# Second layer's down-projection turned to token columns, with DVE block transposes at the end and an earlier scan schedule

## The chip, the cores and the metric

One core of one Trainium2 chip runs the whole program. The metric is device microseconds (us) of one execution; smaller is better. Engines are named as in the profile: PE (TensorE matmul), PEld (its weight load), DVE (VectorE), ACT (ScalarE), SP (the queue from which nearly all DMAs are issued).

## The reference

Three stages follow each other on 12160 tokens (2 sequences of 6080) of width 256:

```python
f = lower_bound + (1 - lower_bound) * sigmoid(f_logit)
h = f[:, t] * h + (1 - f[:, t]) * x[:, t]        # a scan over 6080 steps
y1 = relu(h @ w_in1)**2 @ w_out1                 # 256 -> 2048 -> 256
y2 = elu(y1 @ w_in2) @ w_out2                    # 256 -> 2048 -> 256
```

Weights arrive in 64-bit floats, everything else in 32-bit floats, and the output is 32-bit.

## The kernel before, in words

**Tiling.** Tokens are cut into 24 blocks: 384 tokens, then 23 of 512 (`FIRST`, `block_sizes`). A layer `m` (0 is the squared relu, 1 the elu) treats one block in 8 groups `g` of 256 hidden units. One (layer, block, group) is called a slot here. A float product is made of three matmuls of high and low parts (`(wh,gh)`, `(wh,gl)`, `(wl,gh)`), each pair of parts made by a copy that rounds (`high_part`) and a subtraction (`low_part`). The first four blocks of layer 0 are `plain`: 12 first products of full width. All other slots form the first product from seven half-size products, 9 matmuls named `first` and 12 named `later` (line 626), with sums on DVE around them.

**One slot of layer 1**, engine by engine: PE `first` into a PSUM tile `pc` (2 buffers); ACT `snap` copies three quarters of it (654); PE `later`; DVE `common` (662), `mid_blocks` (669), `pair` (657), `last_block` (665); ACT `first_block` (672), `below` (682), `exp` (685); DVE `elu` (688); ACT `high_part` (693); DVE `low_part` (698), which gives `g` (3 buffers); PE `out_mm` (725), the second product, which stands three slots later in PE's order. Layer 0 has relu and square on ACT in place of `below`, `exp` and `elu`.

**The second product.** For layer 0 weights are stationary and activations move: 12 matmuls with 512 moving columns a slot, results `acc` with output channels on partitions. For layer 1 it is the other way round: 128 tokens of `g` are stationary and 256 columns of `wo` move, 24 matmuls a slot, so that `acc` has tokens on partitions and can be stored as it is: `add_evacuation` moves it by ACT (805) and stores rows of 1 KB (809). Layer 0's result goes through DRAM (`xd`) and comes back by `add_reload`.

**The scan.** `add_scan` works on half a block: four DMAs each for `fs` and `xs` (549, pieces of 256 bytes), tanh on ACT (553), two DVE block transposes to channels on partitions (558), gate, feed, two scans (564, 572, 585). `fs`, `xs`, `fT` and `xT` had one buffer each.

**What sets the order.** Blocks go in pairs; runs of 16 slots alternate between layer 1 of one pair and layer 0 of a pair two ahead, after two runs of layer 0 at the start. `class Order` holds every step with its cost, due time, reads and writes, and lays them out engine by engine with costs of its own (`act`, `dve`, `SAME`, `CROSS`, `LOAD`, `HOLD`); the result is a fixed order in each engine's queue. `SPREAD` says how many slots ahead of its pair's layer-0 run the transposes of each of the four half-block scans are released, so all four fall into the layer-1 run before. I call the runs of layer 1 that have scans to do loaded. Weights are made in the kernel from their 64-bit words (`add_weights`, 383 to 415), those of layer 1 during the first 250 us; `add_sums` and `add_kept_parts` build the seven half-size weights and keep them in DRAM, from where `add_stream` loads them for each run.

Of the kernel before, what the change touches and what calls it, by code (L numbers as in the profile page):

```python
# [7 lines left out]
F32 = mybir.dt.float32  # L8
# [4 lines left out]
ALU = mybir.AluOpType  # L13
# [4 lines left out]
HB = 256  # L18
FIRST = (384,)
LAST = ()  # L20
# [6 lines left out]
START = 12.0  # L27
SPREAD = (15, 11, 8, 4)

BUFS = {  # L30
    "fs": 1, "xs": 1, "fT": 1, "xT": 1, "F": 2, "xA": 1, "xB": 1, "ws": 4, "wp": 3, "r": 3, "e": 1,
    "g": 3, "s": 2, "st": 3, "a": 5, "o": 2, "pc": 2, "acc": 4,
}
# [13 lines left out]
class Order:  # L47
# [8 lines left out]
    RATE, AHEAD = 240.0, 2.0  # L56
    HOLD = 0.2
    SLACK = 0.3
# [35 lines left out]
    def run(self):  # L94
# [33 lines left out]
        while any(ready.values()):  # L128
# [14 lines left out]
            if e == "SP":  # L143
                moved = max(moved, t0 + us / 2) + s[6] / self.RATE
                free[e] = max(free[e], moved - self.AHEAD)
                ends[n] = (e, max(moved, t0 + us))
            else:
                ends[n] = (e, t0 + us)
            for r in ready.values():
# [12 lines left out]
def kernel(  # L162
# [26 lines left out]

    late = ctx.enter_context(tc.tile_pool(name="late", bufs=1))  # L190
    wo1 = late.tile([P, KF, 2, D], F32R, name="wo1")
    pools = {"ws": ctx.enter_context(tc.tile_pool(name="ws_pool", bufs=BUFS["ws"]))}
# [5 lines left out]
    warm = const.tile([P, 1], F32, name="warm")  # L198
    wo = [const.tile([P, KF, 2, D], F32R, name="wo0"), wo1]
    pools |= {  # L200
# [165 lines left out]
    def add_weights(i, m, kind, c, due, wk=None):  # L366
        t = {}

        def load(e):
            t["st"] = new("st", [P, 2, CE // 2, 2], I32)  # L370
            load_w(nc.scalar if i == 0 else nc.sync, t["st"], m, kind, c)
            if i == 0:
                for k in range(KD):
                    nc.scalar.dma_start(lb[:, k : k + 1], lower_bound.rearrange("(q c i o) -> c q i o", q=4, c=KD, o=1)[k])
                nc.scalar.activation(warm, warm, AF.Exp)
            sv = t["st"].rearrange("p k e w -> p (k e) w")
            t["low"], t["high"] = sv[:, :, 0], sv[:, :, 1]
# [19 lines left out]

        def parts():
            if kind == 0:
                return t["a"], ws_t[m, c][:, 0, 0:4], ws_t[m, c][:, 1, 0:4]  # L400
            v = t["a"].rearrange("p (k e) i -> p k (e i)", k=2)
            return v, *(wo[m][:, 2 * c : 2 * c + 2, x, :] for x in range(2))

        def high_part(e):
            if kind == 0:
                ws_t[m, c] = new("ws", [P, 2, NW, P], F32R)
            v, hi, _ = parts()
            if e == "ACT":
                nc.scalar.activation(hi, v, AF.Copy)
            else:  # L410
                nc.vector.tensor_copy(hi, v)

        def low_part(e):
            v, hi, lo = parts()
            nc.vector.tensor_tensor(lo, v, hi.bitcast(F32), op=ALU.subtract)

# [3 lines left out]
        def keep_whole(e):  # L420
# [3 lines left out]
        steps = [  # L424
            ["SP", 0.1 if i == 0 else 1.9 if m == 0 and kind == 0 else 0.475, load, (), [st], None, 512],
            ["ACT", act(CE), scaled, [st], [a]],
# [8 lines left out]
        if m == 1 and kind == 0:  # L435
# [7 lines left out]
            *steps,  # L443
            ["DVE", dve(CE, True), high_part, [a], [w], ("ACT", act(CE))],
            ["DVE", dve(CE), low_part, [a], [w]],
        ])
        if kind == 0:
            order.add("SP", 0.5, due + 6.0, keep, [w], [("wd", m, c, 0)], None, 512)
            order.add("SP", 0.5, due + 3.0, keep_whole, [a], [("rd", c)], None, 256)

# [33 lines left out]
    def add_parts(m, b, ready, due):  # L484
# [132 lines left out]
    def add_slot(i, m, b, g, wk):  # L617
# [82 lines left out]
        def out_mm(e):  # L700
# [3 lines left out]
            for j in (2 * g + 1, 2 * g):  # L704
                d = 0 if j % 2 else 2 * n
                gh, gl = (t["g"][:, x, d : d + 2 * n] for x in range(2))
                one, two = begin and j % 2 == 1, end and j % 2 == 0
                for q in range(KD if m == 0 else 2 * n // P):
                    if m == 0:
                        if one:  # L710
                            acc_t[m, b].append(pa.tile([P, TB], F32, tag="acc", name="acc"))
                        a = acc_t[m, b][q][:, : 2 * n]
                        wh, wl = (wo[0][:, j, x, q * P : (q + 1) * P] for x in range(2))
                        three = ((wh, gh), (wh, gl), (wl, gh))
                        clear = one
                    else:
                        if one and q % 2 == 0:
                            acc_t[m, b].append(pa.tile([P, TB], F32, tag="acc", name="acc"))
                        a = acc_t[m, b][q // 2][:, q % 2 * D : (q % 2 + 1) * D]
                        vh, vl = (x[:, q * P : (q + 1) * P] for x in (gh, gl))  # L720
                        wh, wl = (wo[1][:, j, x, :] for x in range(2))
                        three = ((vh, wh), (vh, wl), (vl, wh))
                        clear = one and q % 2 == 0
                    for k, (u, v) in enumerate(three):
                        nc.tensor.matmul(a, lhsT=u, rhs=v, start=clear and k == 0, stop=two and k == 2, skip_group_check=True)  # L725

        na = KD if m == 0 else -(-2 * n // HB)
        if g == 0:
# [52 lines left out]
    def add_evacuation(m, b):  # L781
        n = sizes[b]
        due = out_due[m, b, KG - 1] + 12 * ROW * n + 4.0
        for q, key in enumerate(acc_k[m, b]):
            if m == 0:
                k = ("o", o_n[0] + q)

# [4 lines left out]
                def spill(e, q=q):  # L792
                    nc.sync.dma_start(xd[b][:, q], o_t[m, b, q])

                chain(due, [
                    ["ACT", act(n, True), move, [key], [k]],
                    ["SP", 0.5, spill, [k], [("xd", b, q)], None, n // 2],
                ])
            else:
                k = ("o", o_n[0] + q)  # L800
                w = min(2, n // P - 2 * q)

                def move(e, q=q, w=w):
                    o_t[m, b, q] = new("o", [P, 2, D])
                    nc.scalar.activation(o_t[m, b, q][:, :w], acc_t[m, b][q].rearrange("p (i e) -> p i e", i=2)[:, :w], AF.Copy)

                def store(e, q=q, w=w):
                    t0 = starts[b] + q * 2 * P
                    nc.sync.dma_start(out[t0 : t0 + w * P, :].rearrange("(i p) e -> p i e", p=P), o_t[m, b, q][:, :w])

                chain(due, [
                    ["ACT", act(w * D, True), move, [key], [k]],
                    ["SP", 0.5, store, [k], (), None, w * 128],
                ])
        o_n[0] += len(acc_k[m, b])

# [104 lines left out]
```

## Time and profile before

| | |
|---|---|
| runs | 2083.47, 2083.7, 2085.03 us, median 2083.7 |
| the profiled execution | 2083.75 us, of which its span is 2082.0 |
| busy in the span | PE 2034.5, PEld 1925.6, DVE 1732.3, ACT 1697.1 us |
| mean granted TensorE clock | 0.996 of 2.4 GHz |
| DMA | 268.10 MB, 16 engines 41.3% busy |

Busy PE is modelled and overlaps, so a share near 100% says that PE is rarely empty, not how fast it goes. How fast it goes is read from the distance between starts of neighbouring groups.

### The profile page before, as it was taken

Reading aid. Unit: us, or ns where it says so; the run is one execution under the profiler, and the core shown is the slowest. Engines: PE = TensorE matmul, PEld = TensorE weight load, DVE = VectorE, ACT = ScalarE, POOL = GpSimd, SP = SyncE. Lnnn points to the kernel's source line nnn. Section 1 sums busy time; section 2 is a strip of 40 time slices with the busy share of each in tenths; the row PEclk is TensorE's granted clock in tenths of the full one; section 3 lists DMA queues with packets and bytes.
Section 4 is the critical chain, followed back from the end, with each engine's and each line's share of the span. In section 5 each row is a group of like instructions: output and inputs, shape, how many; then the busy total and the mean of one; then the engine's idle time right before and its main releaser. Section 6 shows DMA issues by size and latency. Waiting matters only on the chain.

```text
span 2082.0 us, 36897 instructions
## 1 busy us (share of the span) xinstructions
PE 2034.5 (98%) x14640; PEld 1925.6 (92%) x14640; DVE 1732.3 (83%) x2830; ACT 1697.1 (82%) x2149; POOL 0.2 (0%) x4
## 2 busy tenths in 40 slices
PE   3999999999999999999999999999999999999998
PEld 3888889999999999999999999999999999999998
DVE  7977996996897798699699689779869968967876
ACT  5887778888888888889788888888888878888886
POOL 0000000000000000000000000000000000000000
PEclk8999999999999999999999999999999999999999
DMA  8787452442343344334244234334433424423321
GB/s 220 229 258 237 143 173 89 128 131 93 124 141 102 119 116 134 116 108 144 89 124 136 92 124 140 105 119 115 135 117 106 140 90 122 133 92 130 104 95 39
DMA packets 207540, 268.10 MB, mean 129 GB/s; under 512 B 110984, under 2 KB 135944, under 8 KB 207368
## 3 DMA queue, kind: packets, MB, share of 16 engines
q1 hardware_dynamic: 206784, 265.21, 40.7%
q8 instruction: 116, 1.90, 0.4%
q10 hardware_dynamic: 584, 0.53, 0.1%
q14 instruction: 56, 0.46, 0.1%
HBM read 221.91 MB, written 43.78 MB: 128 GB/s over the span
## 4 chain that ended last, share of the span: by engine, by line
PE 93%; DVE 4%; ACT 1%; DMA 1%; issue 0%; SPq 0%; DVEq 0%; ACTq 0%
PE acc L725 49%; PE pc L626 40%; PE pc L640 4%; DVE g L698 1%; DVE r L688 1%; DVE r L669 0%; DMA fs<-in_f_logit_dram 0%; DVE F L585 0%; ACT g L693 0%; DMA a<-rd 0%; DVE s L662 0%; ACT s L654 0%; SPq L328 0%; ACT e L682 0%; DVE r L665 0%
## 5 line engine op out<-in xcount | busy, mean ns | idle before, releaser
L725 PE MATMUL acc<-wo,g 128*128 128x256 f32 x4560 | 579.0, 282 | 4.4 <-DVE g L698 2.6
L725 PEld LDWEIGHTS acc<-wo,g 128*128 128x128 f32 x4560 | 560.1, 188 | 5.9 <-DVE g L698 3.9
L725 PE MATMUL acc<-g,wo 128*128 128x512 f32 (+1 forms) x2304 | 552.6, 389 | 0.0
L725 PEld LDWEIGHTS acc<-g,wo 128*128 128x128 f32 x2304 | 420.9, 188 | 78.5 <-DVE g L698 0.3
L626 PE MATMUL pc<-xB,ws 128*128 128x256 f32 x3696 | 486.9, 280 | 4.4 <-ACT s L654 3.6
L626 PE MATMUL pc<-xA,ws 128*128 128x256 f32 (+1 forms) x3696 | 485.8, 280 | 3.2 <-ACT s L654 2.0
L698 DVE TENSOR_TENSOR g<-r,g 128x1024 fp32r<-128x1024 f32 (+1 forms) x384 | 463.8, 1208 | 27.0 <-ACT g L693 24.7
L626 PEld LDWEIGHTS pc<-xB,ws 128*128 128x128 f32 x3696 | 463.6, 188 | 11.6 <-ACT s L654 4.2
L626 PEld LDWEIGHTS pc<-xA,ws 128*128 128x128 f32 x3696 | 463.0, 188 | 10.2 <-ACT s L654 2.4
L693 ACT ACTIVATE g<-r 128x1024 fp32r<-128x1024 f32 (+1 forms) x384 | 402.1, 1047 | 15.6 <-DVE r L688 8.6
L654 ACT ACTIVATE s<-pc 128x768 f32<-128x768 f32 (+1 forms) x352 | 283.5, 805 | 114.3 <-PE pc L626 112.8
L662 DVE TENSOR_TENSOR s<-pc,s 128x256 f32<-128x256 f32 (+1 forms) x352 | 147.8, 420 | 240.0 <-PE pc L626 238.7
L688 DVE SCALAR_TENSOR_TENSOR r<-e,r 128x1024 f32<-128x1024 f32 (+1 forms) x192 | 231.7, 1207 | 24.4 <-ACT e L685 23.7
L669 DVE TENSOR_TENSOR r<-pc,s 128x512 f32<-128x512 f32 (+1 forms) x352 | 241.8, 687 | 9.3
L682 ACT ACTIVATE e<-r 128x1024 f32<-128x1024 f32 (+1 forms) x192 | 202.0, 1052 | 15.0 <-DVE r L665 6.5
L685 ACT ACTIVATE e<-e 128x1024 f32<-128x1024 f32 (+1 forms) x192 | 202.1, 1052 | 6.0
L678 ACT ACTIVATE r<-r 128x1024 f32<-128x1024 f32 (+1 forms) x192 | 202.2, 1053 | 5.6
L675 ACT ACTIVATE r<-r 128x768 f32<-128x768 f32 x160 | 135.5, 847 | 77.7 <-DVE r L665 76.8
L672 ACT ACTIVATE r<-pc 128x256 f32<-128x256 f32 (+1 forms) x352 | 133.4, 379 | 79.5 <-DVE r L669 66.6
L657 DVE TENSOR_TENSOR s<-s 128x256 f32<-128x256 f32 (+1 forms) x352 | 147.1, 418 | 9.8 <-ACT s L654 0.8
L665 DVE TENSOR_TENSOR r<-s 128x256 f32<-128x256 f32 (+1 forms) x352 | 146.7, 417 | 0.0
L585 DVE TENSOR_TENSOR_SCAN F<-fT,carry,xT 128x256 f32<-128x256 f32 (+2 forms) x94 | 65.7, 728 | 0.3
(49 smaller groups left out, 832.1 us busy)
## 6 DMA issues: line engine op xcount, KB each, us to landing
ws<-wd SPq DMA_DIRECT2D x176, 896.0 KB, 5.0
out_dram<-o SPq DMA_DIRECT2D x47, 256.0 KB, 3.8
fs<-in_f_logit_dram SPq DMA_DIRECT2D x184, 64.0 KB, 3.9
xs<-in_x_dram SPq DMA_DIRECT2D x184, 64.0 KB, 2.1
xd<-o SPq DMA_DIRECT2D x46, 256.0 KB, 2.2
F<-xd SPq DMA_DIRECT2D x46, 256.0 KB, 3.3
st<-in_moe_w_out_dram SPq DMA_DIRECT2D x16, 512.0 KB, 4.6
wd<-wp SPq DMA_DIRECT2D x24, 256.0 KB, 4.0
```

The costliest lines, as they stand in the source:

```text
L626: nc.tensor.matmul(t["pc"][:, c], lhsT=ws[:, p, w], rhs=x_t[m, b][:, r, v], start=(which is FIRST_PRODUCTS and q == 0 and c in (1, 2)), st ...
L654: nc.scalar.activation(t["s"], t["pc"][:, 1:4], AF.Copy)
L657: nc.vector.tensor_tensor(t["s"][:, 1], t["s"][:, 1], t["s"][:, 2], op=ALU.add)
L662: nc.vector.tensor_tensor(t["s"][:, 0], t["pc"][:, 0], t["s"][:, 0], op=ALU.add)
L669: nc.vector.tensor_tensor(t["c"][:, 1:3], t["pc"][:, 2:4], u, op=ALU.add)
L678: nc.scalar.activation(t["r"], t["r"], AF.Square)
L682: nc.scalar.activation(t["e"], t["r"], AF.Relu, scale=-1.0)
L685: nc.scalar.activation(t["e"], t["e"], AF.Exp, scale=-1.0)
L688: nc.vector.scalar_tensor_tensor(t["r"], t["e"], 1.0, t["r"], op0=ALU.subtract, op1=ALU.max)
L693: nc.scalar.activation(t["g"][:, 0], t["r"], AF.Copy)
L698: nc.vector.tensor_tensor(t["g"][:, 1], t["r"], t["g"][:, 0].bitcast(F32), op=ALU.subtract)
L725: nc.tensor.matmul(a, lhsT=u, rhs=v, start=clear and k == 0, stop=two and k == 2, skip_group_check=True)
```

## The change

Layer 1's second product takes layer 0's form: weights stationary, 512 token columns moving, 12 matmuls a slot. For that the 256 columns of `wo[1]` are permuted when its high and low parts are made, in two halves (`parts` returns two pieces), so that DVE transposes of 32 by 32 blocks of `acc` yield tokens on partitions. The result leaves PSUM by four `nc.vector.transpose` a block in place of two ACT copies, and is stored by eight DMAs in pieces of 256 bytes in place of two in rows of 1 KB. `fs` and `xs` get a second buffer, `wp` and `a` lose one each. The first blocks are 512 and 384. `SPREAD` is (16, 13, 10, 7). Rounding copies of weights, and of the inputs of plain blocks, have no DVE alternative any more. ACT loads its table ahead of the first weight DMAs; stores of kept weights are due later; the planner's `HOLD` is 0.1.

```diff
-FIRST = (384,)
+FIRST = (512, 384)
-SPREAD = (15, 11, 8, 4)
+SPREAD = (16, 13, 10, 7)
 BUFS = {
-    "fs": 1, "xs": 1, "fT": 1, "xT": 1, "F": 2, "xA": 1, "xB": 1, "ws": 4, "wp": 3, "r": 3, "e": 1,
-    "g": 3, "s": 2, "st": 3, "a": 5, "o": 2, "pc": 2, "acc": 4,
+    "fs": 2, "xs": 2, "fT": 1, "xT": 1, "F": 2, "xA": 1, "xB": 1, "ws": 4, "wp": 2, "r": 3, "e": 1,
+    "g": 3, "s": 2, "st": 3, "a": 4, "o": 2, "pc": 2, "acc": 4,
-    HOLD = 0.2
+    HOLD = 0.1
...
-                ends[n] = (e, t0 + us)
+                ends[n] = ("SP" if s[6] else e, t0 + us)
...
+            if i == 0:
+                nc.scalar.activation(warm, warm, AF.Exp)
             load_w(nc.scalar if i == 0 else nc.sync, t["st"], m, kind, c)
...
+            hi, lo = (wo[m][:, 2 * c : 2 * c + 2, x, :] for x in range(2))
+            if m == 0:
+                return [(v, hi, lo)]
+            return [
+                (v[:, k].rearrange("p (a q j) -> p q a j", a=4, q=KD),
+                 *(u[:, k].rearrange("p (q a j) -> p q a j", a=4, q=KD) for u in (hi, lo)))
+                for k in range(2)
+            ]
...
-            ["DVE", dve(CE, True), high_part, [a], [w], ("ACT", act(CE))],
+            ["ACT", act(CE), high_part, [a], [w]],
...
-            order.add("SP", 0.5, due + 6.0, keep, [w], [("wd", m, c, 0)], None, 512)
-            order.add("SP", 0.5, due + 3.0, keep_whole, [a], [("rd", c)], None, 256)
+            order.add("SP", 0.5, due + 16.0, keep, [w], [("wd", m, c, 0)], None, 512)
+            order.add("SP", 0.5, due + 10.0, keep_whole, [a], [("rd", c)], None, 256)
...
-                ["ACT", act(4 * n), high(0, 4, 0), ready, [X[0]], ("DVE", dve(4 * n, True))],
+                ["ACT", act(4 * n), high(0, 4, 0), ready, [X[0]]],
...
+                for q in range(KD):
+                    if one:
+                        acc_t[m, b].append(pa.tile([P, TB], F32, tag="acc", name="acc"))
+                    a = acc_t[m, b][q][:, : 2 * n]
+                    wh, wl = (wo[m][:, j, x, q * P : (q + 1) * P] for x in range(2))
+                    for k, (u, v) in enumerate(((wh, gh), (wh, gl), (wl, gh))):
+                        nc.tensor.matmul(a, lhsT=u, rhs=v, start=one and k == 0, stop=two and k == 2, skip_group_check=True)
...
+                def turn(c, h=q):
+                    def go(e):
+                        if c == 0:
+                            o_t[m, b, h] = new("o", [P, HB // 32, KD, 32])[:, : n // 64]
+                        v = acc_t[m, b][c][:, h * n // 2 : (h + 1) * n // 2]
+                        nc.vector.transpose(o_t[m, b, h][:, :, c], v.rearrange("p (n i) -> p n i", i=32))
+                    return go
+                def store(e, h=q):
+                    t0 = starts[b] + h * n // 2
+                    v = out[t0 : t0 + n // 2, :].rearrange("(n j) (a u) -> a j n u", j=32, a=4)
+                    for a in range(4):
+                        nc.sync.dma_start(v[a], o_t[m, b, h][32 * a : 32 * a + 32].rearrange("j n c i -> j n (c i)"))
+                chain(due + 8.0, [
+                    *(["DVE", dve(n // 2), turn(c), [accs[c]], [k]] for c in range(KD)),
+                    ["SP", 1.9, store, [k], (), None, n // 2],
                 ])
```

**What stands where on DVE in a loaded run of layer 1.** The eleventh slot of the run of blocks 4 and 5, from its `common` to the row ahead of the next slot's. Before:

```order
L662 TENSOR_TENSOR s<-pc,s 128x256
L669 TENSOR_TENSOR r<-pc,s 128x512
L657 TENSOR_TENSOR s<-s 128x256
L665 TENSOR_TENSOR r<-s 128x256
L698 TENSOR_TENSOR g<-r,g 128x1024
L585 SCALAR_TENSOR_TENSOR F<-fT,carry,xT 128x256 x2
```

The same slot in the change (670 is `common`, 593 the scan, 696 `elu`, 677 `mid_blocks`, 665 `pair`, 673 `last_block`, 706 `low_part`, 500 to 508 sums for the next block's first product):

```order
L670 TENSOR_TENSOR s<-pc,s 128x256
L593 SCALAR_TENSOR_TENSOR F<-fT,carry,xT 128x256
L696 SCALAR_TENSOR_TENSOR r<-e,r 128x1024
L677 TENSOR_TENSOR r<-pc,s 128x512
L665 TENSOR_TENSOR s<-s 128x256
L673 TENSOR_TENSOR r<-s 128x256
L500 TENSOR_TENSOR F<-F 128x512
L706 TENSOR_TENSOR g<-r,g 128x1024
L599 COPY carry<-F 128x2
L504 TENSOR_TENSOR F<-F 128x256
L508 TENSOR_TENSOR F<-F 128x256
L696 SCALAR_TENSOR_TENSOR r<-e,r 128x1024
```

In the change the fourth and last scan of the run ends here; before, this is the third, and the transposes of the fourth follow in the next slot.

**DVE just after the same run.** Before, the second slot of the layer-0 run that follows, from its `common` on:

```order
L662 TENSOR_TENSOR s<-pc,s 128x256
L516 TENSOR_TENSOR xB<-F,xB 128x768
L657 TENSOR_TENSOR s<-s 128x256
L669 TENSOR_TENSOR r<-pc,s 128x512
L698 TENSOR_TENSOR g<-r,g 128x1024
L665 TENSOR_TENSOR r<-s 128x256
L492 TENSOR_TENSOR F<-F 128x512
```

The same slot in the change:

```order
L670 TENSOR_TENSOR s<-pc,s 128x256
L500 TENSOR_TENSOR F<-F 128x512
L677 TENSOR_TENSOR r<-pc,s 128x512
L706 TENSOR_TENSOR g<-r,g 128x1024
L665 TENSOR_TENSOR s<-s 128x256
L673 TENSOR_TENSOR r<-s 128x256
L504 TENSOR_TENSOR F<-F 128x256
L508 TENSOR_TENSOR F<-F 128x256
L805 STREAM_TRANSPOSE o<-acc 128x8x32 x4
```

The last row is the transposes of the pair's second block; those of its first block stand two and three slots earlier. Before, no instruction of DVE touched `acc`.

**The SP queue from the start.** Before, the first eight rows:

```order
L549 DMA fs<-in_f_logit_dram 32x6x64 x4
L549 DMA xs<-in_x_dram 32x6x64 x4
L328 DMA st<-in_moe_w_in_dram 32x2x512 x8
L549 DMA fs<-in_f_logit_dram 32x6x64 x4
L549 DMA xs<-in_x_dram 32x6x64 x4
L421 DMA rd_140<-a 128x512
L320 DMA st<-in_moe_w_out_dram 128x2x512
L328 DMA st<-in_moe_w_in_dram 32x2x512 x4
```

In the change:

```order
L557 DMA fs<-in_f_logit_dram 32x8x64 x8
L557 DMA xs<-in_x_dram 32x8x64 x8
L557 DMA fs<-in_f_logit_dram 32x6x64 x4
L557 DMA xs<-in_x_dram 32x6x64 x4
L326 DMA st<-in_moe_w_in_dram 32x2x512 x8
L557 DMA fs<-in_f_logit_dram 32x6x64 x4
L557 DMA xs<-in_x_dram 32x6x64 x4
L318 DMA st<-in_moe_w_out_dram 128x2x512
```

Three half blocks of inputs now stand ahead of the second and third group's weights, where one did.

## Rows read from the trace of the kernel before

**Rows 1.** The page: span, and busy time of each engine.
```profile
span 2082.0 us, 36897 instructions
...
PE 2034.5 (98%) x14640; PEld 1925.6 (92%) x14640; DVE 1732.3 (83%) x2830; ACT 1697.1 (82%) x2149; POOL 0.2 (0%) x4
```
**Rows 2.** Waits of PE: engine, line, waited for; us in total, times, longest.
```profile
PE pc L640 <- ACT xA L508: 20.5, 1, 20.5
PE pc L640 <- ACT xB L508: 10.1, 1, 10.1
PE pc L626 <- ACT s L654: 5.6, 5, 1.7
PE acc L725 <- DVE g L698: 2.6, 5, 0.8
```
**Rows 3.** Stretches: start:end, length, busy PE, PEld, DVE, ACT, POOL, clock, DMA.
```profile
54.67:100.00 45.33, 45.33 (x221) 39.88 (x220) 42.56 (x71) 36.86 (x50) 0.00 (x0) 1.00 0.75 232
...
198.20:302.42 104.22, 95.61 (x770) 92.55 (x769) 100.06 (x183) 78.98 (x112) 0.00 (x0) 1.00 0.50 156
...
894.46:980.38 85.92, 85.92 (x721) 85.92 (x721) 83.50 (x136) 73.10 (x93) 0.00 (x0) 1.00 0.43 131
980.38:1063.81 83.43, 83.43 (x530) 75.53 (x530) 58.80 (x98) 68.26 (x87) 0.00 (x0) 1.00 0.33 107
1910.58:1996.50 85.92, 85.92 (x722) 85.92 (x722) 70.48 (x104) 71.17 (x87) 0.00 (x0) 1.00 0.31 104
```
**Rows 4.** Chain of waits in order of time, 894 to 985 and 200 to 330.
```profile
894.46 2.88 PE acc L725 x24
...
313.41 2.75 PE acc L725 x12
```
**Rows 5.** Timeline, end of a loaded run of layer 1.
```profile
963.23 0.42 DVE L662 TENSOR_TENSOR s<-pc,s 128x256 f32<-128x256 f32 x1 [0.18 <-PE pc L626]
...
964.10 3.04 PE L725 MATMUL acc<-wo,g 128*128 128x256 f32 x24
...
969.48 3.04 PE L725 MATMUL acc<-wo,g 128*128 128x256 f32 x24
...
970.40 0.42 DVE L662 TENSOR_TENSOR s<-pc,s 128x256 f32<-128x256 f32 x1
...
972.92 1.22 DVE L698 TENSOR_TENSOR g<-r,g 128x1024 fp32r<-128x1024 f32 x1
974.06 1.22 DVE L516 TENSOR_TENSOR xB<-F,xB 128x1024 fp32r<-128x1024 f32 x1
...
974.84 3.04 PE L725 MATMUL acc<-wo,g 128*128 128x256 f32 x24
```
**Rows 6.** Groups on DVE with shapes kept apart, 894.46 to 980.38.
```profile
L585 DVE TENSOR_TENSOR_SCAN F<-fT,carry,xT 128x256 f32<-128x256 f32 x6 | 4.2, 736 | 0.0
...
L558 DVE STREAM_TRANSPOSE xT<-xs 128x512 f32<-128x512 f32 x3 | 2.1, 704 | 0.0
```
**Rows 7.** Timeline of the start: SP's second load of f_logit, PE's first matmuls.
```profile
10.80 1.80 SPq L549 DMA_DIRECT2D fs<-in_f_logit_dram  x4
...
20.45 0.69 PE L640 MATMUL pc<-xA,ws 128*128 128x384 f32 x1 [20.45 <-ACT xA L508]
...
39.98 0.80 PE L640 MATMUL pc<-xB,ws 128*128 128x512 f32 x1 [10.09 <-ACT xB L508]
...
41.29 5.00 PE L640 MATMUL pc<-xB,ws 128*128 128x512 f32 x11 [0.51 <-DVE xB L516]
```
**Rows 8.** All groups: rounding copies of the weights, on DVE and on ACT.
```profile
L411 DVE CAST wo<-a 128x512 fp32r<-128x512 f32 x15 | 6.4, 424 | 0.4
...
L409 ACT ACTIVATE ws<-a 128x512 fp32r<-128x512 f32 x1 | 0.6, 629 | 0.0
```
**Rows 9.** Timeline of the end: last products, last copies out of PSUM.
```profile
2075.30 2.90 PE L725 MATMUL acc<-wo,g 128*128 128x256 f32 x22 [0.34 <-DVE g L698]
2077.51 1.32 ACT L805 ACTIVATE o<-acc 128x512 f32<-128x512 f32 x2 [3.52 <-PE acc L725]
```

More of the change, by code (lines that the diff above doesn't have):

```diff
@@ L186 @@
     NBK = len(sizes)
-    late = ctx.enter_context(tc.tile_pool(name="late", bufs=1))
-    wo1 = late.tile([P, KF, 2, D], F32R, name="wo1")
     pools = {"ws": ctx.enter_context(tc.tile_pool(name="ws_pool", bufs=BUFS["ws"]))}
@@ L198 @@
     warm = const.tile([P, 1], F32, name="warm")
-    wo = [const.tile([P, KF, 2, D], F32R, name="wo0"), wo1]
+    wo = [const.tile([P, KF, 2, D], F32R, name=f"wo{m}") for m in range(2)]
     pools |= {
@@ L374, in load @@
                     nc.scalar.dma_start(lb[:, k : k + 1], lower_bound.rearrange("(q c i o) -> c q i o", q=4, c=KD, o=1)[k])
-                nc.scalar.activation(warm, warm, AF.Exp)
             sv = t["st"].rearrange("p k e w -> p (k e) w")
@@ L399, in parts @@
             if kind == 0:
-                return t["a"], ws_t[m, c][:, 0, 0:4], ws_t[m, c][:, 1, 0:4]
+                return [(t["a"], ws_t[m, c][:, 0, 0:4], ws_t[m, c][:, 1, 0:4])]
             v = t["a"].rearrange("p (k e) i -> p k (e i)", k=2)
-            return v, *(wo[m][:, 2 * c : 2 * c + 2, x, :] for x in range(2))
+            hi, lo = (wo[m][:, 2 * c : 2 * c + 2, x, :] for x in range(2))
[6 more added lines that the diff above has]
+            ]
         def high_part(e):
@@ L406, in high_part @@
                 ws_t[m, c] = new("ws", [P, 2, NW, P], F32R)
[L407 to L411, printed above, removed]
+            for v, hi, _ in parts():
+                if e == "ACT":
+                    nc.scalar.activation(hi, v, AF.Copy)
+                else:
+                    nc.vector.tensor_copy(hi, v)
         def low_part(e):
-            v, hi, lo = parts()
-            nc.vector.tensor_tensor(lo, v, hi.bitcast(F32), op=ALU.subtract)
+            for v, hi, lo in parts():
+                nc.vector.tensor_tensor(lo, v, hi.bitcast(F32), op=ALU.subtract)
         def keep(e):
@@ L424, in add_weights @@
         steps = [
-            ["SP", 0.1 if i == 0 else 1.9 if m == 0 and kind == 0 else 0.475, load, (), [st], None, 512],
+            ["ACT" if i == 0 else "SP", 5.8 if i == 0 else 1.9 if m == 0 and kind == 0 else 0.475, load, (), [st], None, 512],
             ["ACT", act(CE), scaled, [st], [a]],
@@ L707, in out_mm @@
                 one, two = begin and j % 2 == 1, end and j % 2 == 0
[L708 to L727, printed above, removed]
+                for q in range(KD):
[5 more added lines that the diff above has]
+                        nc.tensor.matmul(a, lhsT=u, rhs=v, start=one and k == 0, stop=two and k == 2, skip_group_check=True)
+        na = KD
         if g == 0:
@@ L783, in add_evacuation @@
         due = out_due[m, b, KG - 1] + 12 * ROW * n + 4.0
-        for q, key in enumerate(acc_k[m, b]):
+        accs = acc_k[m, b]
+        for q in range(KD):
+            k = ("o", o_n[0])
+            o_n[0] += 1
             if m == 0:
-                k = ("o", o_n[0] + q)
                 def move(e, q=q):
@@ L795, in add_evacuation @@
                 chain(due, [
-                    ["ACT", act(n, True), move, [key], [k]],
+                    ["ACT", act(n, True), move, [accs[q]], [k]],
                     ["SP", 0.5, spill, [k], [("xd", b, q)], None, n // 2],
@@ L799, in add_evacuation @@
             else:
[L800 to L813, printed above, removed]
+                def turn(c, h=q):
[13 more added lines that the diff above has]
+                    ["SP", 1.9, store, [k], (), None, n // 2],
                 ])
-        o_n[0] += len(acc_k[m, b])
     def add_reload(b, due):
```

## Prediction

> **What bounds the kernel now.** I read the page first: PE is busy for 98% of the span, DVE and ACT for little over 80% [rows 1]. Then the waits of PE: two at the start, 20.5 and 10.1 us, and beyond them no more than 2.6 to 5.6 us for any cause [rows 2]. So outside the start PE is fed, and its own pace is the time. The table of stretches then shows what stands beside it: a run of 16 slots of layer 1 takes 85.92 us with DVE busy for 83.50 of them, a run of layer 0 takes 83.43 us with DVE busy for 58.80; without scans a layer-1 run takes the same 85.92 us, DVE at 70.48 [rows 3]. The reader is to see that PE sets the length of both runs, and that in the loaded ones DVE has 2.4 us to spare. One stretch differs: from 198 to 302 us DVE is busy for 100.06 of 104.22 us while it makes layer 1's weights and scans [rows 3]. PE is still shown busy there for 95.61, but the pace is DVE's.
>
> I take durations from the profiled execution, 2083.75 us, 0.05 above the median of the runs; 1.75 us of it lie outside the span. A difference of 0.2% is 4.2 us, about what a measurement can tell from none.
>
> **PE's saving.** The chain shows a second product of layer 1 as 24 matmuls in 2.88 us, and one of layer 0 as 12 in 2.75 us [rows 4], for the same number of multiplications: 120 ns for 256 columns against 229 ns for 512. The whole run says a little more: 85.92 - 83.43 = 2.49 us in 16 slots [rows 3], since the first products behind it start a trifle sooner too. Twelve pairs of blocks pass through layer 1; the first of them is DVE's (198 to 302 us) and gains nothing from PE. Eleven runs at 2.49 us are **-27.4 us**.
>
> The Trainium skill speaks against this term. In "TensorE: Matmul & The Clock Gate", section "Back-to-back issue gap", it gives a warm gap of columns / 2.4 + 2.5 ns, by which 24 narrow matmuls and 12 wide ones would differ by 0.03 us a slot, an estimate of 5 us in all in place of 27.4. This trace does not agree: its narrow matmuls stand 13 ns above 256 / 2.4, and layer 0 already runs the wide form with weights and `g` from the same buffers, so I take the rows.
>
> **DVE in the loaded runs.** Nine of the eleven runs have four scans to do. The transposes of the result are new on DVE: four a block of 256 columns. None stands in the trace; a transpose of 512 columns from SBUF takes 0.70 us [rows 6], so half of that is the lower bound and all of it the upper. I take 0.42 us, what `common`, which reads 256 columns of PSUM, takes [rows 5]. The order puts them at the end of the run and into the next, where DVE is idle for 25 of 83 us [rows 3], and `acc` is wanted again only three slots on. ACT is rid of two copies a block. Both cost nothing.
>
> What costs is that scans stand closer. A DVE instruction follows its neighbour some 0.07 us sooner than its duration says (972.92 to 974.06 for 1.22 us [rows 5]). With such steps the order of before gives DVE 61.6 us of work from the slot ahead of a loaded run to its eleventh, 12 slots, in which PE took 5.2 + 11 x 5.37 = 64.3 us. The order of the change has 66.4 us there (two more scans at 0.736 us [rows 6], a transpose, gates and a feed, one more `elu` and the sums for another block), against 12 x 5.215 = 62.6 us of PE. Adding up slot by slot, DVE's lag never passes 1.8 us before; in the change it reaches 3.2 us at the eighth slot and 4.1 at the eleventh. Then it falls: the last five slots are light, so a run as a whole fits.
>
> How much lag does PE bear? At the worst place of before `common` starts at 970.40, 0.92 us behind the start of PE's second product at 969.48; where DVE is on time (963.23) it is 0.87 us ahead of it (964.10), so the lag is 1.8 us, as summed. The `g` made there ends at 972.92 + 1.22 = 974.14, and PE wants it at 974.84 [rows 5]: 0.7 us left, 2.5 us in all. A lag of 4.1 us then stalls PE for 1.6 us a run. Following the two peaks instruction by instruction (`mid_blocks` frees `pc` 0.2 to 0.4 us late, `g` 0.3) gives 0.8. I take 1.2, nine times: **+10.8 us**. Bounds: 0, if DVE makes up the lag as `elu` waits less for ACT, and 9 x 4.1 = 37 us if PE bears none.
>
> **The start.** Before, the second half block's f_logit is issued at 10.80 us, when the first one's buffer is free; PE's first product is at 20.45 us; then PE runs three groups of the first block and waits until 41.29 us for the second block [rows 7]. With two buffers these loads are issued at once. DVE's chain becomes: first scan (256 columns a half) until 15 us, second until 20, PE's first product at 21 to 22 and its second block at about 35.5, when it has also done three groups of 512 columns in place of 384 (36 x 128 columns at 229 / 512 ns, 2 us). That is 6 + 2 = **-8 us**, with -12 and 0 as bounds, for weights of the second group now wait behind three half blocks on SP and could be late themselves.
>
> Two things take some of it back. All rounding copies of weights that DVE did at 0.42 us (15 in the row, 7 more like them) go to ACT at 0.63 us [rows 8], two a group of 9.75 us in the first eight groups: ACT's 36.86 us of 45.33 [rows 3] become 42.7. With tanh and its waits for PE I give this **+3 us** (0 to 8). And from 198 us on DVE, the bound there, gets more: by count of the order 90.3 us for 85.0 between the first and the seventeenth `common`, as `low_part` of layer 1's weights comes in halves and more kept weights are left over; 1.4 us of it are scans that later slots no longer have. **+4 us** (0 to 5.4).
>
> **The end.** After the last product (2078.2) ACT needs 1.3 us for two copies [rows 9], and the store follows. Now four transposes in a row, 1.5 us, and eight DMAs whose issue takes 1.8 us for each four, as on the row at 10.80 [rows 7]: **+2.5 us** (1 to 5).
>
> Sum: 2083.75 - 27.4 + 10.8 - 8 + 3 + 4 + 2.5 = 2068.6 us.
>
> **Rivals.**
>
> *No stall, start kept.* If the lag stays within what PE bears, the sum is 2083.75 - 27.4 - 8 + 1 + 2.5 = 2052 us. For it: PE never waits in a loaded run now. Against it: the lag doubles by count. Chance 0.25.
>
> *DVE takes over the loaded runs.* If stalls are 2.5 us a run, they eat the saving of the nine, and only the two runs without scans and the start gain: 2083.75 - 27.4 + 22.5 - 1 + 2.5 = 2080 us. For it: 83.50 of 85.92 us busy now, and PE wants 83.43. Chance 0.15.
>
> *Slower.* The same place, priced higher: `common` late by the full lag holds `pc`, PE cannot start the slot after next, and ACT's copies behind it slip as well, so that nothing is borne. 4.1 us a run are 37 us: 2083.75 - 27.4 + 37 - 1 + 2.5 = 2095 us. It decides from (27.4 + 1 - 2.5) / 9 = 2.9 us a run on. Chance 0.08.
>
> *The wide form brings nothing in layer 1.* Then runs stay at 85.92 us, DVE is less pressed, and start and end are left: 2083.75 - 1 + 2.5 = 2085 us. Against it: layer 0's rows. Chance 0.04. By the skill's gap, above, it would be 5 us less.
>
> The forecast, with stalls from 0.3 to 2.2 us a run, has 0.48 (2060 to 2078).
>
> **How the numbers follow.** Faster by over 0.2% is below 2079.5: the forecast and the first rival, 0.73, and 0.06 of the second, 0.79. Within 0.2%: 0.09 of the second, 0.03 of the fourth, 0.01 of the slower one, 0.13. Slower: 0.08. The range takes in most of the first rival and the second: 2049 to 2084; below it lies some 0.07, above it 0.1.
>
> **What would show it.** In the changed profile: second products of layer 1 as 12 matmuls in 2.75 us; runs without scans at 83.4 us; loaded runs of 84 to 85.5 us, with PE waiting for `g` or for `pc` once or twice in each, near the eighth and eleventh slots; DVE busy for over 97% of those; PE's second block at 33 to 38 us. Wrong would be: loaded runs at 83.4 (no stall) or at 85.9 and more (DVE the bound); a stretch from 198 us on that shrinks; a transpose from PSUM over 0.7 us.

## The result and the profile after

The changed kernel takes 2063.27 us (median of 4 runs, 2063.02 to 2064.32), the one before 2084.27 beside it: ratio 0.990, 95% interval 0.9883 to 0.9917. The forecast was 2068.6, the range 2049 to 2084. The profiled execution has a span of 2061.4 us, 20.6 less than before.

The page: span, busy time of each engine. PE has fewer instructions, DVE's busy time hardly moves [rows 1].

```profile
span 2061.4 us, 32505 instructions
...
PE 2016.8 (98%) x12384; PEld 1803.6 (87%) x12384; DVE 1724.1 (84%) x2899; ACT 1691.3 (82%) x2144; POOL 0.2 (0%) x4
```

Waits of PE (engine, line, waited for; us in total, times, longest). Of the wait for the second block, 10.1 us before, 1.0 us is left (`xB`); PE now waits 16 times for the `g` that DVE makes, where it waited 5 times [rows 2].

```profile
PE pc L648 <- ACT xA L516: 21.3, 1, 21.3
PE acc L722 <- DVE g L706: 8.1, 16, 1.4
PE pc L634 <- ACT s L662: 4.8, 4, 1.8
PE pc L648 <- DVE xA L524: 1.2, 1, 1.2
PE pc L648 <- DVE xB L524: 1.0, 1, 1.0
```

Stretches from the first second product of a run to that of the next (columns as in [rows 3]): the first run of layer 1, the layer-0 run behind it, a loaded run of layer 1, a run of layer 0, a run of layer 1 without scans. The last two are equal now, 83.41 us; the loaded run is 1.5 us longer.

```profile
202.97:293.88 90.91, 81.57 (x530) 74.29 (x529) 88.68 (x171) 70.19 (x103) 0.00 (x0) 0.99 0.63 180
293.88:377.99 84.11, 84.11 (x529) 76.05 (x529) 60.73 (x105) 69.30 (x89) 0.00 (x0) 0.99 0.35 110
377.99:462.91 84.92, 84.55 (x531) 75.48 (x530) 83.10 (x139) 71.67 (x89) 0.00 (x0) 1.00 0.43 130
462.91:546.32 83.41, 83.41 (x530) 75.53 (x529) 59.11 (x101) 68.45 (x88) 0.00 (x0) 1.00 0.34 109
...
1892.82:1976.24 83.42, 83.42 (x531) 75.54 (x529) 71.58 (x111) 70.89 (x85) 0.00 (x0) 1.00 0.32 108
```

Timeline of PE in that loaded run. A second product without a stall takes 2.75 us to the next start (409.27 to 412.02), and slots without a stall follow each other at 5.21 us. The last two rows are the tenth slot's: after its first matmul it waits for DVE.

```profile
409.27 2.91 PE L722 MATMUL acc<-g,wo 128*128 128x512 f32 x12
412.02 1.57 PE L634 MATMUL pc<-xB,ws 128*128 128x256 f32 x12
...
425.49 0.39 PE L722 MATMUL acc<-g,wo 128*128 128x512 f32 x1
426.17 2.79 PE L722 MATMUL acc<-g,wo 128*128 128x512 f32 x11 [0.29 <-DVE g L706]
```

DVE just before. Two scans and the next block's sums stand between the last two `low_part` (706); the second ends at 424.90 + 1.22 = 426.12, and PE goes on at 426.17.

```profile
419.14 1.23 DVE L706 TENSOR_TENSOR g<-r,g 128x1024 fp32r<-128x1024 f32 x1
420.28 0.75 DVE L593 TENSOR_TENSOR_SCAN F<-fT,carry,xT 128x256 f32<-128x256 f32 x1
...
421.25 0.74 DVE L593 TENSOR_TENSOR_SCAN F<-fT,carry,xT 128x256 f32<-128x256 f32 x1
...
424.30 0.69 DVE L500 TENSOR_TENSOR F<-F 128x512 f32<-128x512 f32 x1
424.90 1.22 DVE L706 TENSOR_TENSOR g<-r,g 128x1024 fp32r<-128x1024 f32 x1
```

Start and end on PE and DVE: the second block is there at 34.62 us (39.98 before, [rows 7]); after the last product (2051.83 + 2.79) come four transposes and the stores.

```profile
21.28 0.79 PE L648 MATMUL pc<-xA,ws 128*128 128x512 f32 x1 [21.28 <-ACT xA L516]
23.25 11.54 PE L648 MATMUL pc<-xA,ws 128*128 128x512 f32 x35 [1.17 <-DVE xA L524]
34.62 0.42 PE L648 MATMUL pc<-xB,ws 128*128 128x384 f32 x1
...
2051.83 2.79 PE L722 MATMUL acc<-g,wo 128*128 128x512 f32 x11 [0.76 <-DVE g L706]
2053.97 1.46 DVE L805 STREAM_TRANSPOSE o<-acc 128x256 f32<-128x256 f32 x4 [2.20 <-PE acc L722]
```

With all stretches cut at the first second product of a run, in us:

| stretch | before | after | gain | predicted |
|---|---|---|---|---|
| start, to layer 1's first second product | 210.38 | 202.97 | -7.4 | -8 + 3 |
| first run of layer 1 | 92.04 | 90.91 | -1.1 | +4 |
| layer 0 behind it | 83.82 | 84.11 | +0.3 | 0 |
| nine loaded runs, each | 85.92 | 84.92 (last 84.72) | -9.2 | 9 x (1.2 - 2.49) = -11.6 |
| nine runs of layer 0, each | 83.43 | 83.41 | -0.2 | 0 |
| first run without scans | 85.92 | 83.41 | -2.5 | -2.49 |
| last run, to its last product's end | 81.86 | 78.38 | -3.5 | -2.49 |
| from there to the end | 3.77 | 6.77 | +3.0 | +2.5 |
| sum | | | -20.6 | -15.1 |

### The profile page after: what moved, and what is told of

It is laid out like the page before. It is cut to its first block, busy times and chain, and to the rows that moved or that the text cites. A ratio compares the mean times of both kernels' runs of the same rounds, so it can differ in the third digit from the quotient of the medians.

```text
span 2061.4 us, 32505 instructions
## 1 busy us (share of the span) xinstructions
PE 2016.8 (98%) x12384; PEld 1803.6 (87%) x12384; DVE 1724.1 (84%) x2899; ACT 1691.3 (82%) x2144; POOL 0.2 (0%) x4
## 4 chain that ended last, share of the span: by engine, by line
PE 61%; DVE 32%; ACT 4%; issue 2%; DMA 0%; SPq 0%; DVEq 0%; ACTq 0%
PE acc L722 32%; PE pc L634 25%; DVE g L706 7%; DVE r L696 6%; DVE r L677 4%; PE pc L648 4%; DVE F L593 3%; DVE s L665 2%; DVE s L670 2%; DVE r L673 2%; DVE fT L572 1%; DVE fT L566 1%; ACT e L693 1%; DVE xT L580 1%; DVE xB L524 1%
## 5 line engine op out<-in xcount | busy, mean ns | idle before, releaser
L722 PE MATMUL acc<-g,wo 128*128 128x512 f32 x4608 | 1115.9, 390 | 9.6 <-DVE g L706 8.1
L722 PEld LDWEIGHTS acc<-g,wo 128*128 128x128 f32 x4608 | 839.3, 188 | 175.0 <-DVE g L706 17.7
L634 PE MATMUL pc<-xA,ws 128*128 128x256 f32 x3696 | 486.5, 280 | 4.1 <-ACT s L662 4.1
L634 PE MATMUL pc<-xB,ws 128*128 128x256 f32 (+1 forms) x3696 | 483.7, 280 | 0.7 <-ACT s L662 0.7
L662 ACT ACTIVATE s<-pc 128x768 f32<-128x768 f32 x352 | 282.4, 802 | 43.7 <-PE pc L634 43.4
L696 DVE SCALAR_TENSOR_TENSOR r<-e,r 128x1024 f32<-128x1024 f32 x192 | 231.0, 1203 | 24.6 <-ACT e L693 23.8
L677 DVE TENSOR_TENSOR r<-pc,s 128x512 f32<-128x512 f32 x352 | 240.4, 683 | 7.4 <-ACT r L680 2.8
L690 ACT ACTIVATE e<-r 128x1024 f32<-128x1024 f32 x192 | 201.6, 1050 | 27.3 <-DVE r L673 22.8
L686 ACT ACTIVATE r<-r 128x1024 f32<-128x1024 f32 x192 | 202.2, 1053 | 4.8
L693 ACT ACTIVATE e<-e 128x1024 f32<-128x1024 f32 x192 | 201.5, 1050 | 4.9
L680 ACT ACTIVATE r<-pc 128x256 f32<-128x256 f32 x352 | 133.8, 380 | 66.4 <-DVE r L677 37.0
```

What stands on the lines that cost most here:

```text
L634: nc.tensor.matmul(t["pc"][:, c], lhsT=ws[:, p, w], rhs=x_t[m, b][:, r, v], start=(which is FIRST_PRODUCTS and q == 0 and c in (1, 2)), st ...
L662: nc.scalar.activation(t["s"], t["pc"][:, 1:4], AF.Copy)
L677: nc.vector.tensor_tensor(t["c"][:, 1:3], t["pc"][:, 2:4], u, op=ALU.add)
L686: nc.scalar.activation(t["r"], t["r"], AF.Square)
L690: nc.scalar.activation(t["e"], t["r"], AF.Relu, scale=-1.0)
L693: nc.scalar.activation(t["e"], t["e"], AF.Exp, scale=-1.0)
```

## The experiments

Below, a run means one of 16 second products, cut as in the table.

**Turned product alone.** The kernel before, with `parts`, `out_mm` and `add_evacuation` of the change.

```diff
-                for q in range(KD if m == 0 else 2 * n // P):
+                for q in range(KD):
...
+                        nc.vector.transpose(o_t[m, b, h][:, :, c], v.rearrange("p (n i) -> p n i", i=32))
```

> The kernel before with the turned product alone (permuted weights, wide matmuls, DVE transposes, new store); scan release, buffers, first blocks as before. By my theory the saving is PE's, 2.49 us in each of 11 runs, and is cut in the nine loaded runs by DVE's lag: by count of the order it peaks at 3.7 us (4.1 in the change), of which PE bears about 2.6, so loaded runs of 84.5 us; the end costs 3 us and the start brings nothing: 2083.7 - 27.4 + 10 + 3 = about 2070. Rival, that half of the change's gain is the start's and the turned product brings little: 2078 or more. Rival, that the lag does not matter: loaded runs of 83.4 us and 2060.

2078.81 us (ratio 0.9976, 0.9966 to 0.9985): a quarter of the gain, and the time that the first rival named. But a run without scans takes 84.37 us, not 83.41, with no wait of PE; 12 wide matmuls take 2.81 us in layer 1 and 2.75 in layer 0. The wide form was slower here than where it is copied from.

**All but the turned product.** The changed kernel with the three functions of before.

> The change with layer 1's second product, its evacuation and its store as before. By my theory what is left is the start: second block at 36 us in place of 41, and the gain of 8.5 us at the start of the first loaded layer-0 run kept to the end; loaded runs stay near 85.9 us (lag peaks at 2.8 us, borne): 2083.7 - 8.5 + 1 = about 2076. Rival, that the start's gain is only there because the first layer-1 run is shorter with wide matmuls: 2080 or more.

2069.0 us (0.9926, 0.9911 to 0.9941): 14.9 us without the product that the change is named for, more than theory and rival expected; the turned product adds some 6 us to it. The start is that of the changed kernel (202.84). The narrow runs without scans take 85.45 us where they took 85.92, again with nothing to see but the pace.

**The place of `wo`.** The change does one thing more, which its list ahead of the prediction leaves out: it takes layer 1's second weights out of a pool of their own (`late`, the first to be allocated) and puts them into the pool of layer 0's, so that they lie elsewhere in SBUF. All but the turned product has this move, the turned product alone has not. These three lines were edited in the turned-alone kernel and in the kernel before; the order on every engine stays the same:

```diff
-    late = ctx.enter_context(tc.tile_pool(name="late", bufs=1))
-    wo1 = late.tile([P, KF, 2, D], F32R, name="wo1")
...
-    wo = [const.tile([P, KF, 2, D], F32R, name="wo0"), wo1]
+    wo = [const.tile([P, KF, 2, D], F32R, name=f"wo{m}") for m in range(2)]
```

> The kernel before with the turned product alone (2078.81 us), and the tile of layer 1's second weights taken from the pool in which those of layer 0 stand, so that it lies elsewhere in SBUF; the instructions and their order stay. With the turned product alone 12 wide matmuls took 2.81 us in layer 1 and 2.75 us in layer 0, and a run of layer 1 without scans 84.37 us where the changed kernel takes 83.41. Theory (the pace of a matmul hangs on where its operands lie in SBUF, here on the place of wo): 12 in 2.75 us, 83.4 us a run without scans, loaded runs 84.1 to 84.4 where they were 85.06, and 2078.8 - 11 x 0.9 = 2069 us (2067 to 2073). Rival (it is the place of other tiles, or DVE and ACT beside it): 2.81 us, 84.3 us, 2077 to 2080 us.

> The kernel before, with nothing but the tile of layer 1's second weights moved to the pool of layer 0's, so that it and the tiles behind it lie elsewhere in SBUF. Turned, this move took a run of layer 1 without scans from 84.37 to 83.41 us. With the narrow form such a run takes 85.92 us in the kernel before and 85.45 in the changed kernel with the product not turned. Theory (the place of wo sets the pace of the narrow products as well): 85.4 to 85.6 us for runs of layer 1, 11 x 0.45 = 5 us less, 2079 us (2077 to 2081). Rival (the narrow form runs at its pace wherever wo lies): 85.9 us, 2083 to 2085 us.

2073.75 us (0.995, 0.9937 to 0.9962) and 2078.62 us (0.9974, 0.9964 to 0.9984). Timeline of PE in a run without scans: turned alone, 2.81 us from start to next start;

```profile
1909.47 2.97 PE L723 MATMUL acc<-g,wo 128*128 128x512 f32 x12
1912.28 1.57 PE L635 MATMUL pc<-xA,ws 128*128 128x256 f32 x12
```

turned with `wo` moved, 2.75 us.

```profile
1990.86 2.91 PE L721 MATMUL acc<-g,wo 128*128 128x512 f32 x12
1993.61 1.57 PE L633 MATMUL pc<-xA,ws 128*128 128x256 f32 x12
```

The narrow form, in the kernel before:

```profile
1910.41 3.04 PE L725 MATMUL acc<-wo,g 128*128 128x256 f32 x24
1913.29 1.58 PE L626 MATMUL pc<-xB,ws 128*128 128x256 f32 x12
...
1915.78 3.04 PE L725 MATMUL acc<-wo,g 128*128 128x256 f32 x24
```

and in the same kernel with `wo` moved:

```profile
1905.09 3.04 PE L723 MATMUL acc<-wo,g 128*128 128x256 f32 x24
1907.97 1.57 PE L624 MATMUL pc<-xB,ws 128*128 128x256 f32 x12
...
1910.43 3.04 PE L723 MATMUL acc<-wo,g 128*128 128x256 f32 x24
```

A run of layer 1 without scans, in us, and in brackets what one of its slots spends on the second product and on the first products, from start to next start:

| | `wo` as before | `wo` moved |
|---|---|---|
| narrow | 85.92 (2.88 + 2.49) | 85.45 (2.88 + 2.46) |
| wide | 84.37 (2.81 + 2.47) | 83.41 (2.75 + 2.46) |

So the 2.5 us are the form's and the place's together, and how they divide hangs on which is changed first: 0.47 for the place and then 2.04 for the form, or 1.55 for the form and then 0.96 for the place. The two gains of the place are not alike. With the wide form the second product got faster, which reads `wo`; with the narrow form the first products did, which do not read it, so there it is the place of some tile that moved along. The granted clock is 1.00 in all four runs.

The expectation of the turned kernel was missed by a little on the loaded runs (84.78, not 84.1 to 84.4) and so on the time (2073.75, not 2067 to 2073). PE gained 0.96 us a run and gave 0.68 of it back in stalls (0.69 us a loaded run before, 1.37 after): with a faster PE and the same order, DVE falls further behind.

**Scans released as before.** `SPREAD` (15, 11, 8, 4) in the changed kernel.

> The change with scans released as before (15, 11, 8, 4). By my theory the loaded runs of the change are 1.5 us longer than PE needs because scans stand too close: here DVE's lag, counted from the order, peaks at 3.0 us in place of 4.1, so stalls of 0.4 us a run in place of 1.5, loaded runs of 83.8 us, and about 2063.3 - 9 = 2054, up to 2058 if the first runs lose by it. Rival, that the sooner release is needed so that the shorter run finds its scans done: loaded runs of 85 us and more, 2065 to 2072. Rival, that the stalls have nothing to do with scans (the transposes, or ACT): 2063.

2065.8 us (0.9914, 0.9897 to 0.993), no faster, and in the band of the first rival. Loaded runs still take 84.94, and 0.27 us more are lost in each layer-0 run behind. The stalls of the 7th and 8th slot stay (5.5 us each), those of the 10th and 12th are gone or nearly so, and others stand at the 14th and 16th (5.4 and 5.85 us). So the release decides where part of the stalls stand, but the earlier one is not what makes a loaded run longer.

**The planner's prices.** The planner is `class Order`, and a price is the cost of a step that it reckons with. A step of a scan takes DVE 0.67 us by the trace, and the planner had 0.43; a gate 0.34 and 0.20. Only these two numbers are changed:

```diff
-            *(["DVE", dve(n, True), gate(c), [("bound",)], [fT]] for c in range(KD)),
+            *(["DVE", dve(n), gate(c), [("bound",)], [fT]] for c in range(KD)),
...
-            *(["DVE", dve(n) + 0.1, scan(c), [fT, xT, ("carry",)] + [("F", u, 0)] * h, [("F", u, h)]] for c in range(KD)),
+            *(["DVE", dve(n) + 0.34, scan(c), [fT, xT, ("carry",)] + [("F", u, 0)] * h, [("F", u, h)]] for c in range(KD)),
```

> The changed kernel, in which the planner that writes the order is told what two DVE instructions of a scan cost by the trace (a scan 0.67 us a step where it had 0.43, a gate 0.34 where it had 0.20); no instruction is added or removed, only the order moves. In the changed kernel a loaded run of layer 1 takes 84.91 us and a run without stalls 83.41; nine loaded runs, so 13.5 us are stalls, and the first run of layer 1 takes 90.9. Theory (the stalls are the order's: scans stand where the planner wrongly thinks DVE idle): loaded runs fall to 83.4 to 83.8 us, the first one to 86 to 89, and the time to about 2045 us (2042 to 2051). Rival (DVE is simply full in a loaded run, 83.1 of 84.9 us busy, so what is taken off one place turns up at another, as with the four smaller release distances): 84.7 to 85.2 us a run, 2062 to 2066 us. Second rival (half of it is seen, as the stall moves to the slots after the run): 2054 to 2058 us.

2051.37 us (0.984, 0.9827 to 0.9854). The stretches of a loaded run and of the first run of layer 1:

```profile
546.68:630.09 83.41, 83.41 (x531) 75.53 (x529) 82.80 (x139) 70.58 (x86) 0.00 (x0) 1.00 0.44 130
208.31:296.43 88.12, 80.36 (x530) 73.42 (x529) 84.24 (x160) 70.37 (x103) 0.00 (x0) 1.00 0.60 168
```

Loaded runs take 83.41 us, as those without scans: no stall is left, though DVE is busy for 82.80 us of it and does the same work. DVE was not full; its order was wrong, with the release as in the changed kernel. Summing DVE's steps (duration less 0.07 us) over the slot ahead of the run and its first eleven gives 66.1 us in the changed kernel and 61.9 here, where PE takes 62.6. The time is above the band of the theory because the start is worse: the first second product of layer 1 comes at 208.31 us.

**One buffer for `fs` and `xs`.** `"fs": 1, "xs": 1` in the changed kernel.

> The changed kernel with one buffer each for fs and xs instead of two. PE's second block starts at 34.6 us in the changed kernel and at 40.0 before; the first second product of layer 1 stands at 203.0 us in the changed kernel and at 210.4 before, which is the gain of the start. Theory (the second buffers make that gain, since the second half block's loads need not wait): second block at 40 to 42 us, the later stretches as in the changed kernel, 2069 to 2072 us. Rival (what makes it is the first block of 512 columns, which gives PE 2 us more to do, and the order of the loads on SP): second block before 37 us, 2063 to 2066 us. Loaded runs stay at 84.9 us in both.

2065.83 us (0.991, 0.9897 to 0.9924): the rival's band by the time, but the place is the theory's. The second block comes at 39.91 us and layer 1's first second product at 207.47, 4.5 us later; but the first run of layer 1 and the layer-0 run behind it are 1.5 and 0.7 us shorter (89.42 and 83.42). The second buffers are worth 4.5 us at the start, and half of that is lost again in the two runs behind it.

**Copies back to DVE.** Weights' and plain blocks' rounding copies get their alternative again.

```diff
-            ["ACT", act(CE), high_part, [a], [w]],
+            ["DVE", dve(CE, True), high_part, [a], [w], ("ACT", act(CE))],
...
-                ["ACT", act(4 * n), high(0, 4, 0), ready, [X[0]]],
+                ["ACT", act(4 * n), high(0, 4, 0), ready, [X[0]], ("DVE", dve(4 * n, True))],
```

> The changed kernel, in which the rounding copies of weights, and of the inputs of plain blocks, may again be put on DVE by the planner (8 more of the weights' copies and some of the inputs' go there). The prediction charged 3 us (0 to 8) for their going to ACT in the first stretch and 4 us (0 to 5.4) for more DVE work in the first run of layer 1. Theory (the charge of 3 us was wrong: ACT had room, and PE is fed from 36 us on either way): first second product of layer 1 at 203 us give or take 1, and 2062 to 2066 us. Rival (ACT's extra work is in the time, hidden by other gains): 2058 to 2061 us. If the copies were what DVE was rid of in the first run of layer 1, that run is longer than 90.9 us by up to 16 x 0.42 = 6.7 us, 2066 to 2070 us.

2060.99 us (0.9887, 0.9873 to 0.99). The start is unmoved (202.92), so the charge of 3 us there was wrong, though the time lies in the rival's band. The gain is in another place than either theory put it: first run of layer 1 89.17 instead of 90.91, the run behind it 83.42 instead of 84.11. That the copies themselves made this gain is not shown: with one buffer for `fs` and `xs`, all copies still on ACT, the same two runs took 89.42 and 83.42.

**Each transpose twice.** In the changed kernel, the planner not told.

```diff
-                        nc.vector.transpose(o_t[m, b, h][:, :, c], v.rearrange("p (n i) -> p n i", i=32))
+                        for _ in range(2):
+                            nc.vector.transpose(o_t[m, b, h][:, :, c], v.rearrange("p (n i) -> p n i", i=32))
```

> The change with every transpose of the result done twice. By my theory the transposes fall where DVE has slack: the four more of each block cost nothing in the loaded runs, and 1.4 us at the end: 2064 to 2066. Rival, that DVE's total sets the loaded runs: 8 times 0.35 us more in each of nine runs, 2063.3 + 25 = 2088.

2088.63 us (1.0019, 1.001 to 1.0029), 25 us more: the theory is refuted, and the time is the rival's. The stalls inside the loaded run stay as they were; new ones (slots of 5.78 and 6.27 us) stand at the seam to the layer-0 run, where the transposes are. The eight transposes more in a pair of blocks are 2.8 us of DVE, and 2.0 of them come into each pair of runs.

**The gains together.** True prices from the fifth half block on (so that the start keeps its order), copies back, and every second store of the last block on ACT's queue. The run beside it has the prices from the second half block on.

```diff
+            *(["DVE", dve(n, i < 4), gate(c), [("bound",)], [fT]] for c in range(KD)),
...
+            *(["DVE", dve(n) + (0.34 if i >= 4 else 0.1), scan(c), [fT, xT, ("carry",)] + [("F", u, 0)] * h, [("F", u, h)]] for c in range(KD)),
...
+                        (nc.scalar if b == NBK - 1 and a % 2 else nc.sync).dma_start(v[a], o_t[m, b, h][32 * a : 32 * a + 32].rearrange("j n c i -> j n (c i)"))
```

> The changed kernel with three edits, each seen in a stretch of its own. The planner has the trace's prices of scan and gate from the fifth half block on (with them from the first on, loaded runs took 83.41 us and not 84.91, but the start came 5.3 us later than in the changed kernel); rounding copies may go to DVE again (the first run of layer 1 took 89.17 us with that, not 90.91); of the last block's eight stores, four are issued from ACT's queue (the end, from the last product on, takes 6.77 us; SP issues four of them in 1.9). Theory (the three gains add): first second product of layer 1 at 203 us, loaded runs 83.41, the first run 87 to 89, the end 5 us; 2061.0 - 9 x 1.5 - 1.9 = 2045.6 us (2043 to 2048). Rival (the early start and the steady order exclude each other, since DVE's work is only shifted into the first run): that run at 92 to 94 us, 2050 to 2053 us.

> As the run beside it, but with the trace's prices from the second half block on, so that the order of the start is another again. Where the second half block's scan is priced dear in the start, PE's second block came at 37.5 us and its first second product at 42.6, in place of 34.6 and 38.0. Theory (that delay comes from the price of the very first scan, which now is the old one): first second product of layer 1 at 203 us, 2044 to 2048 us. Rival (it comes from the second to fourth): at 206 to 209 us, 2048 to 2052 us.

2046.81 us (0.9822, 0.9809 to 0.9836) and 2049.01 us (0.983, 0.9816 to 0.9843). Stretches of the first kernel: a loaded run and the first run of layer 1.

```profile
542.79:626.21 83.42, 83.42 (x531) 75.58 (x530) 82.82 (x139) 70.51 (x86) 0.00 (x0) 1.00 0.43 130
203.19:292.55 89.36, 80.64 (x530) 73.43 (x529) 87.81 (x169) 71.67 (x106) 0.00 (x0) 1.00 0.60 178
```

Start at 203.19, loaded runs at PE's pace, the end 5.61 us instead of 6.77 (2039.21 to 2044.82). This is 16.5 us faster than the changed kernel and the fastest here. In the other kernel the start is at 203.78: what delayed it by 5.3 us was the price of the very first half block's scan, as the theory had it. The time is in the rival's band even so, as its first run (90.58) and the one behind (84.25) are longer.

**Transposes twice, with the prices true.** The kernel of 2046.81 us, transposes doubled and priced double.

> The run that puts the three gains together (2046.81 us), with each transpose of the result done twice, and the planner told so (its price doubled). In the changed kernel the same doubling, with the price as it was, cost 25 us: 2.8 us of DVE a pair of blocks, of which 2.0 came into the time. The prediction said that the transposes cost nothing in the runs. Theory (they cost nothing where the order is made with prices that are true, since a run of layer 0 leaves DVE idle for 26 of 83.4 us): all runs at 83.41 us, the end 1.5 us longer for the second four transposes, 2047 to 2050 us. Rival (DVE work at the seam of two runs costs time wherever it is put, as DVE is busy for 82.9 of the 83.4 us ahead of it): 2 us a pair of blocks, 2066 to 2072 us.

2062.73 us (0.9897, 0.9881 to 0.9914): between the bands of theory and rival. Inside the loaded run nothing stalls, but one slot at the seam takes 6.20 us; 1.2 us a pair of runs, where the unpriced doubling cost 2.0. The first two runs, the last ones and the end take the rest. The true price helps, and the seam has no room for 2.8 us more.

## Why the prediction was right, and where not

The time fell within the range and near the forecast, and the parts that it named (a faster PE that gives some of its gain back in stalls behind DVE, a shorter start, a longer end) are what the table shows. That it came so near is in part luck: the loaded runs gained 2.4 us less than forecast, while the start, with ACT's copies, and the first run of layer 1 gained 7.5 us more. Step by step:

- **PE's saving**, 2.49 us a run: right in size, 2.5, and this too is in part luck. It was read as the form's alone. The prediction took layer 0's rows as the price of the wide form, with weights "from the same buffers"; but in the kernel before, `wo` of layer 1 lay in a pool of its own. Had the change left it there, 1.55 us a run would have come. The last run gave 1.0 us more than this; that lies in its last four slots (17.4 us before, 15.8 after), and all but the turned product has it as well (15.8). The second product itself took 2.88 us before and 2.75 after, 0.13 us less a slot. The Trainium skill's formula ("TensorE: Matmul & The Clock Gate", section "Back-to-back issue gap") gave an estimate of 0.03 us for it; the section states the formula for an isolated matmul, and says that in a stream it counts too little for few columns and too much for many, so it did not speak against the term in the way that the prediction says. The 229 ns of 512 columns here are above its 216.
- **Stalls**, 1.2 us in each of nine runs: 1.5. The slots that take longer are the 7th, 8th, 10th and 12th of the run (5.45, 5.54, 5.77 and 5.58 us from one second product to the next), where 8 and 11 were foreseen, and the 66.4 us counted for the twelve slots are 66.1. The count of DVE's work against PE's time holds: with 61.9 us in the twelve slots nothing stalls. What fails is the cause, that "scans stand closer", where it means their earlier release: with the release of before a loaded run is no shorter, with true prices the stalls go at the changed kernel's release. The planner put scans where it wrongly held DVE for idle.
- **The start**, -8: -7.4, with the second block at 34.6 us (33 to 38 foreseen). One buffer less costs 4.5 of it; the rest (the first block of 512 columns, the loads' order) was not taken apart. **ACT's copies**, +3: nothing in the start. With the copies put back, the first run of layer 1 and the one behind it are 1.7 and 0.7 us shorter, but other orders give that too.
- **The first run of layer 1**, +4: -1.1, the largest miss, and one of the signs that the prediction itself named as showing it wrong. The count between two `common` said 5.3 us more of DVE work; in the trace, with the run cut at second products, DVE is busy for 88.68 us there and was for 89.52 before (the stretch below, which begins later than that of [rows 3]). With the turned product alone that run grows by 1.2 us (93.27), and all else takes 2.2 off (89.82). So the term for the turned product seems to be there, and smaller; but this run differs by as much from one order to the next. That DVE's share of work bounds this run is not shown either: with true prices it is 88.12 us. How short it could be stays open.

```profile
210.38:302.42 92.04, 84.17 (x695) 82.28 (x694) 89.52 (x160) 69.39 (x97) 0.00 (x0) 1.00 0.47 146
```

- **The transposes**: 0.42 us assumed, 0.426 measured. "Both cost nothing" holds for four a block in the order of the changed kernel, and for no more than that, as the doubled ones show. With the turned product alone, whose last scan is released later and meets them, the stall of a loaded run stands at this seam (its 16th slot takes 5.96 us, the others 5.27); which of the two makes it was not taken apart.

```profile
L805 DVE STREAM_TRANSPOSE o<-acc 128x256 f32<-128x256 f32 x92 | 35.7, 426 | 2.2 <-PE acc L722 2.2
```

- **The end**, +2.5: +3.0. With half of the stores on another queue it is 1.2 us shorter.

The rival of no stalls, 2052 us, was within reach: two numbers in the planner make it 2051.4. The rival by which DVE takes over the loaded runs is refuted: they go at PE's pace with DVE busy for 99% of them.

## What to carry to other kernels

A busy share of 98% on a second engine does not say that it bounds; ask first whether its order was made with prices that the trace confirms, since two corrected numbers were worth 12 us here, over half of what the whole change was. When a price is taken from another place of the same kernel, as layer 0's for layer 1, look at what else differs there, the place of the operands too. Time won ahead of a stretch that lags is partly lost in it, so sum by stretches.

## What was not expected of the hardware

The pace of matmuls hung on where tiles lie in SBUF. With nothing else changed, the order and the granted clock the same, 12 wide matmuls took 2.81 or 2.75 us, 234 or 229 ns each, and a run of the narrow form 85.92 or 85.45 us; over the whole kernel some 5 us in either form. The move of `wo` shifts the tiles allocated behind it too, and in the narrow form the gain was in matmuls that do not read `wo`. So which tile sets the pace, and why, is open.
